# Two halves of the first weight block on one queue, and an activation load that waits for the identity

## The chip, the cores and the metric

The kernel runs on one core of a Trainium2 chip. A core has five engines with instruction streams of their own: TensorE (PE in the profile; its weight loads are PEld), VectorE (DVE), ScalarE (ACT), GpSimd (POOL) and SyncE (SP). SyncE and ScalarE issue the DMA transfers in this kernel, each on its own queue (SPq and ACTq in the profile). The metric is the time of one execution on the device in microseconds (us); lower is better. The median of three runs before the change is given below.

## The reference

The reference prunes the weight matrix 2:4 and multiplies: in each group of four consecutive rows of w, column by column, the two entries of largest magnitude are kept.

```python
# x: (16, 512, 1024), w: (1024, 1024), b: (1024,), all bf16
wg = w.reshape(G, M, D)                      # M = 4
mag = jnp.abs(wg)
order = jnp.argsort(mag, 1)
thr = jnp.take_along_axis(mag, order[:, M - N:M - N + 1, :], 1)   # N = 2
wp = (wg * (mag >= thr)).reshape(D, D)
return jnp.einsum("bsd,df->bsf", x, wp) + b
```

So there are 8192 tokens (64 tiles of 128), 1024 input features and 1024 output columns.

## The kernel before

**Tiles.** The contraction over 1024 features is cut into two groups g of 512; within a group, partition q holds four consecutive rows (m = 0 to 3) of w, so that one group of four lies in one partition and pruning is elementwise work on VectorE. `w_sb` is the raw weight, `wp` the pruned one in this layout, and `wp_nat` the pruned one in natural row order, which the DMA queues make from `wp` (calls `W0.0` and the like).

**The opening stage.** Weights are pruned in six pieces: four of 256 columns for g = 0, two of 512 columns for g = 1. Piece 0 is what everything starts with; its raw weights come as two loads of 128 KB, rows m = 0, 1 (first half) and m = 2, 3 (second half). While pieces are pruned, the first seven token tiles (0 to 6) are loaded in plain layout (`load_x`; tiles 3 and 4 are one load of 256 KB, 5 and 6 one, 2 one of 128 KB, 0 and 1 one), transposed on TensorE against an identity matrix (L193, tokens `T3a` and so on; four 128-column transposes to a tile), copied out of PSUM by ScalarE (L198, `C3a` and so on) and multiplied with each pruned piece as soon as it is there (L229, `M3.0yp`: tile 3, piece 0, rows y = m 2 and 3, columns p = the left half). Later tiles come transposed by DMA (L112, L237, L411) and use `wp_nat` (L242); these are 88% of the time.

**Pruning a piece** on VectorE: `abs` (L169, sign bit masked off; `abs0a` for the first half of piece 0, `abs0b` for the second), `hi` and `lo` (maximum and minimum within each of two pairs), `t1`, `t2` and `thr` (the second largest of the four), `mask` (`is_ge`) and `mult` (the write into `wp`). `hi0a` reads the pair that the first half holds, `hi0b` that of the second; `lo0` before the change does both pairs in one instruction. The `abs` of pieces 2 and 3 is done by ScalarE (L162), behind its copies.

**What sets the order.** Each engine's sequence in the opening is written out by hand in `order`, a list of tokens for each of "pe", "dve", "act" and "sp"; `run` emits them engine by engine, and `seq` keeps each engine's instructions in that sequence. Before that list, TensorE runs `filler` matmuls on constants that write a PSUM bank nobody reads: six of 512 columns and fourteen of 128 (L138). The transposes are next in TensorE's order, `T3a` first. The loads that stand ahead of the list are issued in the order of the calls, on SyncE by default and on ScalarE where the call says "act". ScalarE's first calculation is `spark` (L121), one element, which brings in its function table. `make_identity` (GpSimd) builds the identity.

Of the kernel before, what the change touches and what calls it, by code (L numbers as in the profile page):

```python
# [11 lines left out]
def kernel(  # L12
# [7 lines left out]
    nc = tc.nc  # L20
    P = 128
    bf16 = mybir.dt.bfloat16
# [32 lines left out]
    const = ctx.enter_context(tc.tile_pool(name="const", bufs=1))  # L55
# [11 lines left out]
    def seq(eng, inst):  # L67
        if eng in tails:
            tc.add_manual_dep(inst.ins, tails[eng].ins.name, NOSYNC, reason="program order")
        tails[eng] = inst  # L70
        return inst

    def pe(i):
        return seq("pe", i)
# [4 lines left out]
    def act(i):  # L79
        return seq("act", i)  # L80
# [4 lines left out]
    def pool(i):  # L85
        return seq("pool", i)
# [9 lines left out]
    def issue(eng, out_, in_):  # L96
        q = nc.sync if eng == "sp" else nc.scalar
        return seq(eng, q.dma_start(out_, in_))

    def load_w(g, c0, c1, ma=0, mb=4, eng="sp"):  # L100
        issue(eng, w_sb[:, g, ma:mb, c0:c1], wv[:, g, ma:mb, c0:c1])

    def load_x(ta, tb, eng="sp"):
        xs = const.tile([P, tb - ta, HK], bf16, name=f"x_{ta}")
        issue(eng, xs[:], xf[ta * P:tb * P, :HK].rearrange("(t p) k -> p t k", p=P))
        for t in range(ta, tb):
            x_sb[t] = xs[:, t - ta, :]
# [7 lines left out]

    xnat, held = {}, {}

    load_w(0, 0, 256, 0, 2)
    load_w(0, 0, 256, 2, 4, "act")
    load_x(5, 7, "act")  # L120
    act(nc.scalar.activation(spark[:], nc.const_aps.tensor(1.0, [P, 1], bf16), Act.Abs))  # L121
    load_x(3, 5)
    load_x(2, 3)
    load_w(0, 256, 512)
    load_x(0, 2)
    load_w(0, 512, 768)
# [2 lines left out]
    xnat.update(load_lead(0))  # L129
    pieces = [(0, 0, 256), (0, 256, 512), (0, 512, 768), (0, 768, 1024), (1, 0, 512), (1, 512, 1024)]  # L130

    ident = const.tile([P, P], bf16)
    make_identity(nc, ident[:])
    warm_ps = psum_o.tile([P, FH], fp32, name="ps")

    def filler(n, rep=1):
        for _ in range(n):
            pe(nc.tensor.matmul(warm_ps[:, :rep * P], lhsT=nc.const_aps.tensor(1.0, [P, P], bf16),  # L138
                                rhs=nc.const_aps.tensor(1.0, [P, rep * P], bf16), start=True, stop=True))
# [119 lines left out]
    def stage(key):  # L259
        solo = key[1] == "h"  # L260
        q, h, at = (pair_of[key[0]], key[2], int(key[0] != SOLO)) if solo else (key[0], key[1] // 2, key[1] % 2)
        if (q, h) not in staged:
# [12 lines left out]
        ),  # L275
        "dve": (
# [4 lines left out]
        ),  # L281
        "act": (
            "C3a C4a C5a C6a C2a S0b0 C0a C1a abs2 S3b0 S2b0 abs3 S0b1 U6h0 S3b1 S2b1 S0b2 S3b2 S2b2 S0b3 U6h1 S3b3 "
# [107 lines left out]
    def run(queues):  # L391
        while any(queues.values()):
            moved = False
            for eng, toks in queues.items():
                while toks and all(n in written for n in needs(eng, toks[0])):
                    emit(eng, toks[0])
                    tok = toks.pop(0)
                    written.add(tok)
                    if tok[0] == "M" or tok[0].islower():
                        written.update(atoms(tok))  # L400
                    moved = True
            assert moved, queues

    filler(6, 4)
    filler(14)
    run({eng: order[eng].split() for eng in order})

    def load_nat(ta, tb):
# [117 lines left out]
```

## Time and profile before

| What | us |
|---|---|
| median of three runs | 232.86 (232.36 to 233.05) |
| the profiled execution | 232.89 |
| its span, first to last instruction | 231.1 |
| TensorE busy in the span | 226.6 |
| VectorE busy | 107.9 |
| ScalarE busy | 14.0 |
| GpSimd busy | 17.6 |

The profile is of one execution. A row of its timeline gives the start in us from the beginning of the span, the us it lasted, the engine, the line of the kernel, the operation, what is written and read, and how often; several instructions of a kind in a row are merged into one line. What stands in brackets is how long the engine sat idle before and what ended that. Busy time of TensorE counts matmuls that overlap in its pipeline, so the pace is read from distances between starts. A DMA has two lines: one in the timeline, of the issuing engine's time, and one in the list of issues, with the us from issue to landing.

### The profile page before, as it was taken

The page shows a single profiled execution, that of the slowest core. Times are in us where ns is not written, and L with a number is a line of the kernel's source. Part 1 is how long each engine was busy: PE and PEld are TensorE (multiplying, and loading weights), DVE is VectorE, ACT ScalarE, POOL GpSimd, SP SyncE. Part 2 cuts the span into 40 slices and gives each one's busy share as a digit, 9 for nine tenths or more (in the row PEclk, how much of TensorE's full clock was granted, in tenths as well). Part 3 has the DMA queues.
Part 4 walks back from the last instruction along what each step waited for, and adds up shares of the span by engine and source line. Part 5 has one row for each costly group of instructions (what it writes and reads, how often), then busy time and mean ns, then how long its engine had stood idle before and what let it go on. Part 6 is the DMA issues. An engine that isn't in the chain of part 4 may idle for free.

```text
span 231.1 us, 2851 instructions
## 1 busy us (share of the span) xinstructions
PE 226.6 (98%) x1142; PEld 110.9 (48%) x1162; DVE 107.9 (47%) x200; ACT 14.0 (6%) x27; POOL 17.6 (8%) x15
## 2 busy tenths in 40 slices
PE   8999999999999999999999999999999999999995
PEld 5986444444444444444444444444444444444443
DVE  3999877844424424424424424423423423433434
ACT  2874100000000000000000000000000000000000
POOL 1000199700000000000000000000000000000000
PEclk9999999999999999999999999999999999999999
DMA  6999999997399422991259821693128932122122
GB/s 203 276 197 280 164 217 223 297 320 252 124 206 232 155 91 72 237 281 64 75 116 252 222 94 71 162 298 134 65 91 198 273 122 83 54 91 91 53 86 91
DMA packets 79308, 38.19 MB, mean 165 GB/s; under 512 B 64192, under 2 KB 71744, under 8 KB 79296
## 3 DMA queue, kind: packets, MB, share of 16 engines
q1 hardware_dynamic: 68384, 20.75, 43.6%
q10 hardware_dynamic: 10912, 17.27, 20.9%
q8 instruction: 9, 0.15, 0.3%
q14 instruction: 3, 0.02, 0.0%
HBM read 3.28 MB, written 16.78 MB: 87 GB/s over the span
## 4 chain that ended last, share of the span: by engine, by line
PE 98%; issue 0%; DVE 0%
PE ps L242 88%; PE ps L229 5%; PE tp L242 2%; PE ps L138 2%; PE tp L193 1%; PE ps L193 0%; DVE o L437 0%
## 5 line engine op out<-in xcount | busy, mean ns | idle before, releaser
L242 PE MATMUL ps<-wp_nat,xb 128*128 128x512 bf16 (+1 forms) x831 | 178.9, 375 | 0.9
L242 PEld LDWEIGHTS <-xb 128*128 128x128 bf16 x848 | 82.2, 98 | 97.7
L437 DVE TENSOR_TENSOR o<-ps,bias_sb 128x512 bf16<-128x512 f32 (+1 forms) x112 | 71.6, 677 | 113.7 <-PE ps L242 111.4
L433 POOL TENSOR_TENSOR st<-st,bias_sb 128x1024 f32<-128x1024 f32 x8 | 16.7, 2142 | 0.0
L242 PE MATMUL ps<-wp_nat,xlead 128*128 128x512 bf16 x63 | 14.7, 379 | 0.1
L242 PEld LDWEIGHTS <-xlead 128*128 128x128 bf16 x88 | 8.6, 98 | 10.2
L229 PE MATMUL ps<-wp,xt 128*128 128x256 bf16 (+1 forms) x130 | 12.8, 258 | 0.0
L439 DVE TENSOR_TENSOR o<-ps,st 128x512 bf16<-128x512 f32 x16 | 11.1, 691 | 2.8 <-PE ps L242 2.2
L229 PEld LDWEIGHTS <-xt 128*128 128x128 bf16 x130 | 10.9, 98 | 1.1
L242 PE MATMUL ps<-wp_nat,xlow 128*128 128x512 bf16 x47 | 10.6, 379 | 0.1
L264 ACT COPY st<-ps 128x512 f32<-128x512 f32 x14 | 7.4, 600 | 3.2 <-PE ps L229 3.1
L242 PEld LDWEIGHTS <-xlow 128*128 128x128 bf16 x48 | 4.7, 98 | 5.7
L159 DVE TENSOR_TENSOR mag<-mag,hi 128x256 bf16<-128x256 bf16 (+2 forms) x15 | 6.1, 435 | 0.1
L159 DVE TENSOR_TENSOR wp<-w_sb,mag 128x256 bf16<-128x256 bf16 (+2 forms) x15 | 6.1, 435 | 0.1
L242 PE MATMUL tp<-wp_nat,xlead 128*128 128x512 bf16 x23 | 5.8, 380 | 0.0
L138 PE MATMUL ps<-const-bfloat16-1.0 128*128 128x128 bf16 (+1 forms) x20 | 4.2, 408 | 0.8 <-PEq L510 0.8
L169 DVE TENSOR_SCALAR mag<-w_sb 128x512 uint16<-128x512 uint16 (+2 forms) x5 | 2.3, 473 | 3.5 <-DMA w_sb<-in_w_dram 3.5
L138 PEld LDWEIGHTS <-const-bfloat16-1.0 128*128 128x128 bf16 x20 | 2.3, 146 | 2.4 <-issue 2.4
L159 DVE TENSOR_TENSOR hi<-mag 128x512 bf16<-128x512 bf16 (+2 forms) x7 | 3.2, 458 | 0.1
L159 DVE TENSOR_TENSOR lo<-mag 128x512 bf16<-128x512 bf16 (+1 forms) x6 | 3.1, 509 | 0.0
L193 PEld LDWEIGHTS <-x 128*128 128x128 bf16 x28 | 2.3, 124 | 0.3 <-DMA x<-in_x_dram 0.2
L422 POOL COPY pruned<-wp 128x1 bf16<-128x1 bf16 x1 | 0.2, 187 | 26.7 <-DVE wp L159 26.7
(18 smaller groups left out, 18.8 us busy)
## 6 DMA issues: line engine op xcount, KB each, us to landing
out_dram<-o ACTq DMA_DIRECT2D x58, 256.0 KB, 2.4
wp_nat<-wp SPq DMA_DIRECT2D x14, 128.0 KB, 3.2
out_dram<-o ACTq DMA_DIRECT2D x10, 128.0 KB, 1.7
w_sb<-in_w_dram SPq DMA_DIRECT2D x2, 512.0 KB, 5.5
w_sb<-in_w_dram SPq DMA_DIRECT2D x3, 256.0 KB, 5.1
x<-in_x_dram SPq DMA_DIRECT2D x2, 256.0 KB, 4.3
x<-in_x_dram ACTq DMA_DIRECT2D x1, 256.0 KB, 4.0
bias_sb<-in_b_dram SPq DMA_DIRECT2D x1, 256.0 KB, 4.7
```

The source lines that it names most:

```text
L138: pe(nc.tensor.matmul(warm_ps[:, :rep * P], lhsT=nc.const_aps.tensor(1.0, [P, P], bf16), rhs=nc.const_aps.tensor(1.0, [P, rep * P], bf16), ...
L159: dve(nc.vector.tensor_tensor(out, a, b_, op=op))
L169: dve(nc.vector.tensor_single_scalar(mag.bitcast(u16), w_.bitcast(u16), 0x7FFF, op=Alu.bitwise_and))
L193: pe(nc.tensor.transpose(tp[:, m, :], xg[:, m, :], ident[:]))
L229: pe(nc.tensor.matmul(ps[:, c0 + d:c1 + d], lhsT=xpk[t][:, m, :], rhs=wp[:, g, m, c0:c1], start=(new and m == ms.start), stop=(left[key] = ...
L242: pe(nc.tensor.matmul(ps, lhsT=xt[:, kt - koff, :], rhs=wp_nat[:, kt, c0:c1], start=(kt == first), stop=(kt == last)))
L264: act(nc.scalar.copy(staged[(q, h)][:, at, :, :].rearrange("p t c -> p (t c)"), ps_open.pop(key)[:]))
L422: pool(nc.gpsimd.tensor_copy(out=pruned[:], in_=wp[:, 1, 3, Dout - 1:]))
L433: pool(nc.gpsimd.tensor_tensor(st[:], st[:], bias.to_broadcast([P, 2, 2, CW]), op=Alu.add))
L437: dve(nc.vector.tensor_tensor(o[:, c0:c1], ps, bias_sb[:, c0:c1], op=Alu.add))
L439: dve(nc.vector.tensor_tensor(o[:, c0:c1].rearrange("p (n c) -> p n c", n=2), ps.rearrange("p (n c) -> p n c", n=2), add, op=Alu.add))
```

## The change

Five things are edited.

- The second half of piece 0's weights is loaded on SyncE's queue, right behind the first half, and no longer on ScalarE's.
- ScalarE's loads are now those of tiles 3 and 4 and of tile 2, and both stand behind `spark`; the load of tiles 5 and 6 goes to SyncE. Thus SyncE issues: first half, second half, tiles 5 and 6, piece 1, tiles 0 and 1, pieces 2 and 3, and the first of g = 1.
- Before the load of tiles 3 and 4, GpSimd copies one column of the identity into the tile that the load will fill; the identity is built ahead of the loads for that.
- VectorE's order for piece 0 begins `abs0a hi0a abs0b lo0a lo0b hi0b`: one instruction more, and `hi0a` ahead of the second half's `abs`.
- Three of the fourteen short fillers are gone.

```diff
     def load_x(ta, tb, eng="sp"):
         xs = const.tile([P, tb - ta, HK], bf16, name=f"x_{ta}")
+        if ta == 3:
+            pool(nc.gpsimd.tensor_copy(out=xs[:, 0, :1], in_=ident[:, :1]))
         issue(eng, xs[:], xf[ta * P:tb * P, :HK].rearrange("(t p) k -> p t k", p=P))
...
+    ident = const.tile([P, P], bf16)
+    make_identity(nc, ident[:])
     load_w(0, 0, 256, 0, 2)
-    load_w(0, 0, 256, 2, 4, "act")
-    load_x(5, 7, "act")
+    load_w(0, 0, 256, 2, 4)
     act(nc.scalar.activation(spark[:], nc.const_aps.tensor(1.0, [P, 1], bf16), Act.Abs))
-    load_x(3, 5)
-    load_x(2, 3)
+    load_x(3, 5, "act")
+    load_x(5, 7)
+    load_x(2, 3, "act")
     load_w(0, 256, 512)
...
-    ident = const.tile([P, P], bf16)
-    make_identity(nc, ident[:])
...
-            "abs0a abs0b hi0a lo0 hi0b t20 t10p t10q thr0p thr0q ..."
+            "abs0a hi0a abs0b lo0a lo0b hi0b t20 t10p t10q thr0p thr0q ..."
...
     filler(6, 4)
-    filler(14)
+    filler(11)
```

8 rows, old and new, of the table order are left out of this document.

## The prediction

> **What bounds the kernel now.** I read the page first (shares and the chain that ended last), then the waits of the whole run, then TensorE's timeline of the opening.
>
> ```profile
> span 231.1 us, 2851 instructions
> PE 226.6 (98%) x1142; PEld 110.9 (48%) x1162; DVE 107.9 (47%) x200; ACT 14.0 (6%) x27; POOL 17.6 (8%) x15
> PE 98%; issue 0%; DVE 0%
> ...
> PE ps L138 <- PEq L510: 0.8, 1, 0.8
> PEld L193 <- DMA x<-in_x_dram: 0.2, 1, 0.2
> ```
>
> The chain is TensorE from one end to the other. In the list of all waits TensorE stands twice: 0.8 us at the start of the program, and 0.2 us before its first transpose, for a load of x. After that transpose it waits for nothing until the end. So a delay of that transpose shifts the end by as much, and so does a gain, as long as no other wait appears.
>
> ```profile
> 0.77 4.21 PE L138 MATMUL ps<-const-bfloat16-1.0 128*128 128x512 bf16 x20 [0.77 <-PEq L510]
> 4.96 1.04 PE L193 MATMUL tp<-ident,x 128*128 128x128 bf16 x8
> 5.80 0.72 PE L193 MATMUL ps<-ident,x 128*128 128x128 bf16 x8
> 6.35 0.39 PE L193 MATMUL tp<-ident,x 128*128 128x128 bf16 x4
> 6.58 1.92 PE L229 MATMUL ps<-wp,xt 128*128 128x128 bf16 x20
> 3.29 1.43 PEld L138 LDWEIGHTS <-const-bfloat16-1.0 128*128 128x128 bf16 x13 [0.28 <-issue]
> 4.96 1.62 PEld L193 LDWEIGHTS <-x 128*128 128x128 bf16 x20 [0.24 <-DMA x<-in_x_dram]
> ```
>
> Two things are to be seen. Fillers end and the load of tiles 3 and 4 lands (1.24 plus 3.7, rows below) at 4.9, and the transposes start at 4.96. And the pace changes: the first eight transposes start within 0.84 us (5.80 less 4.96, 0.105 each), the last four within 0.23 (0.0575 each). The eight between take 0.55: x at 0.105 and 8-x at 0.0575 gives x of about 2. So ten transposes, 1.05 us, ran at about half clock, and the full clock came at 6.0, some 5.2 us after the first filler. Each us of work at the slow pace costs 0.45 us (1 less 0.0575/0.105); these cost 0.48.
>
> **The change, part by part: ScalarE's load.** The order of the built program tells more than the diff. Its rows for the new kernel:
>
> ```
> ACT  L124 LoadActFuncSet
> ACT  L124 Activation spark<-const-bfloat16-1.0 128x1
> ACT  L98 DMACopy x_91<-in_x_dram 128x2x512 [waits DMAHW1_49,Pool_49]
> ACT  L98 DMACopy x_96<-in_x_dram 128x512 [waits DMAHW2_49]
> DVE  L171 TensorScalarPtr mag_145<-w_sb 128x512 [waits DMAHW1_49]
> PE   L195 Ldweights x_3_91 [waits DMAHW1_49,Pool_49]
> ```
>
> Eight completion semaphores (0 to 7) are dealt out to the loads in turn. SyncE's first eight loads take all eight, since the wait for the identity puts ScalarE's loads behind them, and none of the eight waits. The load of tiles 3 and 4 then gets number 1 again, the one for which the second `abs` (the fifth row) waits: that of the second weight half. So it waits for GpSimd's copy and also for the landing of that half. Tile 2's load gets number 2 and waits for tiles 5 and 6, which are SyncE's third.
>
> ```profile
> 0.73 0.45 SPq L98 DMA_DIRECT2D w_sb<-in_w_dram  x1
> 1.24 0.96 SPq L98 DMA_DIRECT2D x<-in_x_dram  x2
> 2.25 0.68 SPq L98 DMA_DIRECT2D w_sb<-in_w_dram  x1
> 0.74 0.50 ACTq L98 DMA_DIRECT2D w_sb<-in_w_dram  x1
> 1.26 0.49 ACTq L98 DMA_DIRECT2D x<-in_x_dram  x1
> 1.79 1.28 ACT L121 ACT_TABLE_LOAD   x1 [1.79 <-issue]
> 1.01 0.29 POOL masks.py:199 TENSOR_SCALAR_AFFINE_SELECT ident<-ident 128x128 bf16<-128x128 bf16 x1
> w_sb<-in_w_dram SPq DMA_DIRECT2D x1, 128.0 KB, 2.7
> w_sb<-in_w_dram ACTq DMA_DIRECT2D x1, 128.0 KB, 2.9
> x<-in_x_dram SPq DMA_DIRECT2D x1, 256.0 KB, 3.7
> x<-in_x_dram ACTq DMA_DIRECT2D x1, 256.0 KB, 4.0
> out_dram<-o ACTq DMA_DIRECT2D x58, 256.0 KB, 2.4
> ...
> 2.60:4.78 2.18, 2.18 (x17) 1.58 (x14) 1.28 (x6) 0.68 (x2) 0.00 (x0) 1.00 1.02 345
> ```
>
> The issue rows are those of the single loads: the weight halves at 0.73 and 0.74 took 2.7 and 2.9 us, tiles 3 and 4 at 1.24 took 3.7, tiles 5 and 6 at 1.26 took 4.0. The windows row ends with the bytes that all queues moved: 345 GB/s.
>
> *Release.* GpSimd's copy is no limit: the identity is done at 1.30, and the table load, now first on ScalarE at 0.74, ends near 2.0. The second half is issued at 1.24, where the x load stood; with its 2.7 us it lands at 3.94. On the other side, both halves had landed by 3.64 (0.74 plus 2.9) with the same bytes, and the first at about 3.5 (below). I take 3.7, nearer the second, because no x is now ahead of it; ends 3.5 and 3.94.
>
> *Flight.* A load of 256 KB issued at that point meets SyncE's backlog (six loads behind the halves). The first half's 2.7 us holds 128 KB; the other 128 KB cost 0.38 us at 345 GB/s and 0.76 at half of it. So 3.1 to 3.5, and I take 3.3. Ends: the 2.4 of a store of that size, and the 4.0 of ScalarE's load.
>
> Tiles 3 and 4 thus land at 3.7 + 3.3 = 7.0 (ends 5.9 and 7.9), where the first transpose started at 4.96: **+2.04 us**. The fillers are over by then, and nothing else stands ahead in TensorE's order: `T5a`, whose load may be there, is queued behind `T3a`.
>
> *Tile 2.* Tiles 5 and 6 landed at 5.3 (1.26 plus 4.0); with 256 KB fewer ahead of them (0.76 us at 345 GB/s) about 4.5. Tile 2 then needs 2.7 for 128 KB: 7.2, or 8.0 if no byte is saved. Its transpose is due sixteen transposes after 7.0, at 7.9 at the fast pace. I take 0; ends 0 and 0.1.
>
> **Fillers.** Thirteen took 1.43 us, so three are 0.33 us, and TensorE would be free at about 4.5. In front of the landing at 7.0 that gains nothing; before the change, too, the load ended that wait. Their price is in the clock: work stops after 3.7 us of it (0.77 to 4.5), where the full clock had come after 5.2. If the clock is full when the transposes start, the 0.48 us come back: **-0.48**. If it isn't, see the second rival.
>
> **VectorE's order.**
>
> ```profile
> 3.50 0.49 DVE L169 TENSOR_SCALAR mag<-w_sb 128x512 uint16<-128x512 uint16 x2 [3.50 <-DMA w_sb<-in_w_dram]
> 4.11 0.42 DVE L159 TENSOR_TENSOR lo<-mag 128x512 bf16<-128x512 bf16 x1
> 4.45 0.28 DVE L159 TENSOR_TENSOR hi<-mag 128x256 bf16<-128x256 bf16 x1
> 4.65 0.28 DVE L159 TENSOR_TENSOR lo<-lo 128x256 bf16<-128x256 bf16 x1
> 5.80 0.48 DVE L159 TENSOR_TENSOR wp<-w_sb,mag 128x256 bf16<-128x256 bf16 x2
> 7.01 0.42 DVE L169 TENSOR_SCALAR mag<-w_sb 128x1024 uint16<-128x1024 uint16 x1
> 9.47 1.06 ACT L162 ACTIVATE mag<-w_sb 128x1024 bf16<-128x1024 bf16 x1
> 10.56 0.43 DVE L159 TENSOR_TENSOR lo<-mag 128x512 bf16<-128x512 bf16 x1
> ```
>
> The whole `lo0` occupies 0.34 us until the next start, a half-size step 0.20: two halves cost 0.40, so +0.06. If the second half lands at 3.94, `abs0b`, `lo0a`, `lo0b`, `hi0b` follow at 0.20 each, and `t20` starts at 4.74 instead of 4.65: +0.09 at most. An earlier first half can give about as much back. The first product is written at 5.80 to 6.1, and TensorE's first matmul on it moves from 6.58 to above 8: two us of cover, so I cost this at 0 (without the cover, 0.09).
>
> Piece 1's weights keep their issue slot at 2.25, so `abs1` at 7.01 stands. From piece 2 on VectorE is tied to TensorE: its `lo2` at 10.56 follows ScalarE's `abs2` (9.47 plus 1.06), which stands behind ScalarE's copies of transposed tiles and so moves with them. Both sides shift together: no further cost, no recovery.
>
> **Sum.** 232.89 (the profiled execution, 0.03 above the median) + 2.04 - 0.48 = 234.45, given as 234.4.
>
> **Rivals.**
>
> *The clock is not open when the transposes start.* TensorE idles from 4.5 to 7.0, and the first 1.8 us of fillers had not opened it (they lay before 2.6, and the pace stayed slow). Then between 1.05 us of work, as before, and 5.2 us, the whole count anew, run slowly; in the middle 3.1. At 0.45 that is 1.40, less the 0.48 already in the old time: 232.89 + 2.04 + 0.92 = 235.9 (234.9 to 236.8). Against it: 3.7 us of fillers may be enough.
>
> [...]
>
> *The landing is cheap.* Release at 3.5 and the store's 2.4 us: transposes at 5.9, 232.89 + 0.94 - 0.48 = 233.35, within 0.3% of the time before. Against it: no load of the opening took under 2.7 us, even for half the bytes.
>
> *Faster, by an earlier full clock.* If the gate opens during the fillers, all twenty transposes run fast, and 0.48 us are won. It decides if tiles 3 and 4 start before 4.96 + 0.48 = 5.44; for 0.3% faster before 4.74, and at 4.6 it gives 232.05. The release at 3.5 or later leaves 1.1 us for 256 KB; the shortest row is 2.4. I see little for it.
>
> *The wait does nothing.* If the semaphore is long met when ScalarE gets there (by 2.2), the load lands at 2.2 + 3.1 = 5.3 and the time is 232.89 + 0.34 - 0.48 = 232.75: no change. Against it: VectorE's first `abs` waited for weights until 3.50.
>
> **How the numbers follow.** A measurement of this kernel tells about 0.3% (0.7 us) from no change. Forecast as reckoned, 233.6 to 234.9: 0.50. Clock still shut, 234.9 to 236.8: 0.33. A late flight beside a shut clock, beyond 236.8: 0.03. Cheap landing: 0.06. Faster: 0.04. The wait does nothing: 0.04. So faster 0.04, same 0.10 (the cheap landing and the idle wait), slower 0.86. The range goes from 233.5 to 236.6: it leaves out the last two cases, most of the cheap landing, and the upper end of the shut clock.
>
> **What would show it.** Right: the first transpose starts near 7.0, its wait of about 2.5 us ended by the DMA of x; ScalarE's issue of that load stands near 3.7, right behind the start of VectorE's second `abs`; no later wait of TensorE. The clock shows in the transposes' spacing: 0.0575 or 0.105. Wrong: ScalarE's issue near 2, a first transpose before 5.5, or a later gap on TensorE where VectorE or tile 2 comes too late.

## The result, and the profile after

The changed kernel takes 239.14 us (median of four runs, 238.28 to 239.56) against 232.72 for the kernel before: 2.75% slower, the ratio being 1.0275 with a 95% interval of 1.0255 to 1.0296. The profiled execution took 238.28, with a span of 236.5. The direction was forecast; the 234.4 us were not, and the time lies above the range.

The page's shares and chain of the changed kernel, then rows from the list of its waits:

```profile
span 236.5 us, 2869 instructions
PE 95%; DMA 3%; SPq 0%; issue 0%; DVE 0%; ACTq 0%
...
PE tp L195 <- DMA x<-in_x_dram: 4.7, 1, 4.7
DVE lo L161 <- ACT mag L164: 5.6, 1, 5.6
```

DMA is now 3% of the chain that ended last, and TensorE waits 4.7 us for a load of x before its first transpose. There is no other new wait of TensorE. VectorE's 5.6 us before piece 2's `lo` is the tie to ScalarE's `abs2`: it has the time to spare.

TensorE's timeline of the opening, with ScalarE's DMA issues and the issue-to-landing rows of the loads issued at 0.73, 1.24, 1.75, 2.25, 2.97 (SyncE) and 3.54 (ScalarE; these are single loads, one at a time):

```profile
0.78 3.89 PE L140 MATMUL ps<-const-bfloat16-1.0 128*128 128x512 bf16 x17 [0.78 <-PEq L512]
9.40 1.02 PE L195 MATMUL tp<-ident,x 128*128 128x128 bf16 x8 [4.73 <-DMA x<-in_x_dram]
10.21 1.06 PE L195 MATMUL ps<-ident,x 128*128 128x128 bf16 x8
11.06 0.63 PE L195 MATMUL tp<-ident,x 128*128 128x128 bf16 x4
11.49 2.44 PE L231 MATMUL ps<-wp,xt 128*128 128x128 bf16 x20
13.76 0.39 PE L195 MATMUL tp<-ident,x 128*128 128x128 bf16 x4
3.54 1.54 ACTq L98 DMA_DIRECT2D x<-in_x_dram  x2
w_sb<-in_w_dram SPq DMA_DIRECT2D x1, 128.0 KB, 2.3
w_sb<-in_w_dram SPq DMA_DIRECT2D x1, 128.0 KB, 2.2
x<-in_x_dram SPq DMA_DIRECT2D x1, 256.0 KB, 3.0
w_sb<-in_w_dram SPq DMA_DIRECT2D x1, 256.0 KB, 3.4
x<-in_x_dram SPq DMA_DIRECT2D x1, 256.0 KB, 5.1
x<-in_x_dram ACTq DMA_DIRECT2D x1, 256.0 KB, 5.7
```

The second weight half, issued at 1.24, lands at 3.46, and ScalarE issues the load of tiles 3 and 4 at 3.54. That is the semaphore wait. The load then flies 5.7 us, to 9.26, and the first transpose starts at 9.40 where it had started at 4.96: 4.44 us. All twenty transposes run at 0.106 us each, and so does the work behind them until 12.55, when the clock opens; 3.15 us are slow, where 1.05 were before. The 2.10 more cost 0.45 each, 0.95. Together 5.39, which is the whole difference of the two profiled executions (238.28 less 232.89).

The median lies 0.9 above this execution. Each run's span comes with its mean granted clock. It is 1.0 for this run, in which nothing was recorded before the clock opened at 12.55, and 0.986 for the other three: by an estimate from that mean (1.4% of 237.5 us, twice) some 6.7 us at half clock. Run e4 below, with the same mean, shows such a course in a trace.

### The profile page after: what moved, and what is told of

The parts are those of the page before. It is cut to its first block, busy times and chain, and to the rows that moved or that the text cites. A ratio compares the mean times of both kernels' runs of the same rounds, so it can differ in the third digit from the quotient of the medians.

```text
span 236.5 us, 2869 instructions
## 1 busy us (share of the span) xinstructions
PE 228.3 (97%) x1159; PEld 111.7 (47%) x1159; DVE 108.0 (46%) x201; ACT 14.3 (6%) x27; POOL 17.8 (8%) x16
## 4 chain that ended last, share of the span: by engine, by line
PE 95%; DMA 3%; SPq 0%; issue 0%; DVE 0%; ACTq 0%
PE ps L244 86%; PE ps L231 5%; DMA x<-in_x_dram 2%; PE tp L244 2%; DMA w_sb<-in_w_dram 1%; PE tp L195 1%; PE ps L195 0%; SPq L98 0%; DVE o L439 0%; ACTq L98 0%
## 5 line engine op out<-in xcount | busy, mean ns | idle before, releaser
L244 PE MATMUL ps<-wp_nat,xb 128*128 128x512 bf16 (+2 forms) x848 | 179.8, 375 | 0.0
L231 PE MATMUL ps<-wp,xt 128*128 128x256 bf16 (+1 forms) x130 | 13.3, 264 | 0.0
L231 PEld LDWEIGHTS <-xt 128*128 128x128 bf16 x130 | 11.5, 102 | 1.2
L195 PE MATMUL tp<-ident,x 128*128 128x128 bf16 x16 | 2.0, 288 | 4.7 <-DMA x<-in_x_dram 4.7
L161 DVE TENSOR_TENSOR lo<-mag 128x512 bf16<-128x512 bf16 (+2 forms) x7 | 3.1, 459 | 5.7 <-ACT mag L164 5.6
```

The source lines that it names most:

```text
L161: dve(nc.vector.tensor_tensor(out, a, b_, op=op))
L195: pe(nc.tensor.transpose(tp[:, m, :], xg[:, m, :], ident[:]))
L231: pe(nc.tensor.matmul(ps[:, c0 + d:c1 + d], lhsT=xpk[t][:, m, :], rhs=wp[:, g, m, c0:c1], start=(new and m == ms.start), stop=(left[key] = ...
L244: pe(nc.tensor.matmul(ps, lhsT=xt[:, kt - koff, :], rhs=wp_nat[:, kt, c0:c1], start=(kt == first), stop=(kt == last)))
```

## The experiments

All edits are of the changed kernel unless said otherwise. The medians of the kernel before, taken beside them, were 232.45 (the first four), 232.44 (the next four) and 232.76 (the last three).

**e1: without the copy, and so without the wait**

```diff
-        if ta == 3:
-            pool(nc.gpsimd.tensor_copy(out=xs[:, 0, :1], in_=ident[:, :1]))
```

> The changed kernel without GpSimd's copy into the tile of 3 and 4. The built order then gives ScalarE's load of tiles 3 and 4 a fresh semaphore and no wait; everything else of the change stays. Theory 1 (the reused semaphore is the cause: the load waited until 3.5 for the second weight half): the load is issued at about 2.2 us, behind the table load, lands 3.1 to 4.0 us later, first transpose between 5.3 and 6.2, time 233.0 to 235.0, depending on the clock. Rival (putting that load on ScalarE's queue behind the table load, or the DVE order, is the cause, and the wait is incidental): first transpose still after 8, time still above 237.5.

Measured: 233.57 us, ratio 1.0045 (1.003 to 1.006), within the range expected. ScalarE's and TensorE's rows, VectorE's second `abs`, and the loads issued at 0.80 (ScalarE) and 1.25 (SyncE):

```profile
0.73 1.28 ACT L122 ACT_TABLE_LOAD   x1 [0.73 <-PEq L510]
0.80 0.98 ACTq L98 DMA_DIRECT2D x<-in_x_dram  x2
4.46 0.97 PE L193 MATMUL tp<-ident,x 128*128 128x128 bf16 x8
5.88 0.64 PE L193 MATMUL ps<-ident,x 128*128 128x128 bf16 x8 [0.45 <-DMA x<-in_x_dram]
7.32 1.92 PE L229 MATMUL ps<-wp,xt 128*128 128x128 bf16 x20 [0.58 <-DVE wp L159]
5.02 0.29 DVE L169 TENSOR_SCALAR mag<-w_sb 128x512 uint16<-128x512 uint16 x1 [0.75 <-DMA w_sb<-in_w_dram]
x<-in_x_dram ACTq DMA_DIRECT2D x1, 256.0 KB, 3.4
w_sb<-in_w_dram SPq DMA_DIRECT2D x1, 128.0 KB, 3.8
```

5.6 us of the loss go with the wait. Two steps behind the expected time failed, both usefully. ScalarE did not issue its load at 2.2 but at 0.80, while the table load was running (0.73 to 2.01): here the table load, of 1.28 us, didn't hold up the DMA issue that stands behind it. And the load, issued 0.45 us before the second weight half on the other queue, landed 0.8 us ahead of it (4.2 against 5.0; the second half took 3.8 us instead of 2.2). VectorE's second `abs` waits until 5.02, and TensorE waits 0.58 us for the first pruned weights. The place taken early in the line was the second half's. So the time fell into its range by two misses that offset each other: the transposes began at 4.46 and not at 5.3 or later, and TensorE then waited 0.45 and 0.58 us.

**e2: 40 more fillers.** `filler(40)` behind `filler(11)`.

> The changed kernel with 40 more short fillers, so that TensorE goes on working until about 7.5 to 8.7 us and the load of tiles 3 and 4 still lands last (9.3 us). The wait isn't touched. Theory (3.15 us of the work after the first transpose ran at half clock because TensorE stood idle from 4.5 to 9.4): the clock is full at the first transpose, the transposes are 0.056 us apart, and 0.45 x 3.15 = 1.4 us come back: 237.7 us. Rival (the clock's opening doesn't hang on the fillers): transposes at 0.105 us, time 239.1.

Measured: 237.32 us (236.78 to 238.64), ratio 1.0196 (1.0178 to 1.0214). That is near the 237.7, but the one trace doesn't show the course expected. It is of the slowest execution (238.64): the clock opens at 3.68, the fillers end at 6.63 (8.55 less 1.92), the first transposes stand at 8.55 at the fast pace (0.056 us apart), and at 10.50 the clock is taken back:

```profile
8.55 0.61 PE L195 MATMUL tp<-ident,x 128*128 128x128 bf16 x8 [1.92 <-DMA x<-in_x_dram]
10.48 0.61 PE L195 MATMUL tp<-ident,x 128*128 128x128 bf16 x4 [0.87 <-DMA x<-in_x_dram]
0.27:3.68 3.41, 2.91 (x10) 1.00 0.47 105
7.09:10.50 3.41, 1.08 (x17) 1.00 1.10 330
10.50:13.92 3.42, 3.42 (x23) 0.50 1.21 232
```

The last three rows are windows: length, TensorE's busy us, matmul count, granted clock, DMA share and GB/s. (The profile gives 1.00 also for the time before the first recorded opening.) This execution's mean clock is 0.993; the other four, 236.78 to 237.43 us, have 0.999 or 1.0, so none of them records such a stretch of 3.4 us at half clock. They may well have kept the clock, as expected; no trace of them shows it. In addition tile 2 is late, see e9.

**e3 and e4: what makes the flight long.** Both release the load by data: the copy into its tile reads the second weight half, not the identity. e3 holds back SyncE's loads of pieces 2 to 4 and the first transposing load, by a GpSimd copy from tile 3 into piece 2's weights; e4 holds only the transposing load, by one into `xlead`.

```diff
-            pool(nc.gpsimd.tensor_copy(out=xs[:, 0, :1], in_=ident[:, :1]))
+            pool(nc.gpsimd.tensor_copy(out=xs[:, 0, :1], in_=w_sb[:, 0, 3, :1]))
...
+    pool(nc.gpsimd.tensor_copy(out=w_sb[:, 0, 0, 512:513], in_=x_sb[3][:, :1]))
     load_w(0, 512, 768)
```

This is e3; e4 has, in place of the last edit:

```diff
+    pool(nc.gpsimd.tensor_copy(out=xlead[:, 0, P:P + 1], in_=x_sb[3][:, :1]))
     xnat.update(load_lead(0))
```

> The changed kernel with the load of tiles 3 and 4 released by the second weight half through data (GpSimd copies one column of that half, not of the identity, into the tile), so the release stays at 3.5 to 3.9 us; and SyncE's later loads (pieces 2, 3, 4 and the first transposing load) held back until tiles 3 and 4 have landed, by a GpSimd copy from tile 3 into piece 2's weights. Theory (the 5.7 us flight is SyncE's backlog): flight 2.4 to 3.5 us, first transpose at 6.3 to 7.3, time 235 to 237. Rival (ScalarE's queue is slow by itself, or one of the 16 DMA engines is): flight 5 us or more, first transpose at 9 or later, time 238.5 or more.

> As the run before, but only the first transposing load of SyncE's queue is held back until tiles 3 and 4 have landed; the three weight loads ahead of it stay. Release by the second weight half through data. If the transposing load causes the long flight: first transpose at 6.5 to 7.5. If the plain weight loads cause it: first transpose at 9 or later, time about 239.

Measured, one run each: e3 236.81 us, flight 4.1, first transpose at 8.05; e4 238.81 us, flight 4.8, first transpose at 8.78. Both first transposes lie between the forecasts. So the transposing load is not the cause, and SyncE's loads issued behind ours account for a part at most: without any of them the flight was still 4.1 us. The windows of e4, and for comparison two of the changed kernel:

```profile
0.63:4.04 3.41, 3.27 (x14) 1.00 0.57 152
4.04:7.45 3.41, 0.39 (x6) 1.00 1.00 257
7.45:10.86 3.41, 2.08 (x20) 0.50 1.05 328
10.86:14.28 3.42, 3.42 (x23) 0.50 1.10 215
```

```profile
2.31:5.72 3.41, 2.36 (x14) 1.00 0.98 251
9.14:12.55 3.41, 3.15 (x29) 1.00 1.18 227
```

In e4 the clock opened at 4.04 during the fillers, was taken back at 7.45 in the wait, and came again only at 14.28, after 5.5 us of slow work. That is a run with two half-clock stretches of 3.41 us; its mean clock is 0.986, as in the three runs above.

**e7: the same place in the line, on the other queue.** No copy, no wait; tiles 3 and 4 are SyncE's sixth load, tile 2 its seventh.

> Tiles 3 and 4 issued on SyncE as the sixth load, at about 3.6 us (where ScalarE issued it in the changed kernel), with no wait and no copy; tile 2 behind it. Theory A (place in the line of issue sets the landing, not the queue): flight 3.4 us or more, first transpose at 7.0 to 8.5, time 235 to 238. Rival B (ScalarE's queue was the slow one): flight under 3.0 us, as SyncE's third load had in the changed kernel, first transpose before 6.6.

Measured: 237.2 us (one run), as forecast for the place in the line. The load, issued at 3.62, and the transposes:

```profile
x<-in_x_dram SPq DMA_DIRECT2D x1, 256.0 KB, 4.6
8.26 1.04 PE L193 MATMUL tp<-ident,x 128*128 128x128 bf16 x8 [3.59 <-DMA x<-in_x_dram]
```

A flight of 4.6 and a start at 8.26: as late as from ScalarE (e3 8.05, e4 8.78) with no semaphore in play. So, with issues at 3.62 us from SyncE (flight 4.6) and at 3.81 from ScalarE (e3, flight 4.1), it is the moment of issue that makes the landing late, not ScalarE's queue.

**e5: the wait for the identity kept, the reused semaphore avoided**

```diff
+    pool(nc.gpsimd.tensor_copy(out=w_sb[:, 0, 0, 512:513], in_=ident[:, :1]))
     load_w(0, 512, 768)
```

> The changed kernel with one more GpSimd copy, of a column of the identity into piece 2's raw weights, ahead of SyncE's load of that piece. That load is issued at 3.6 anyhow, so the copy delays nothing, but now only five SyncE loads stand ahead of ScalarE's load of tiles 3 and 4 in the dealing of semaphores: it gets a fresh one and waits for the identity copy alone. Theory A (the whole loss is the reused semaphore; and loads of both queues are served as one line in the order of issue): issue at 1.6, third or fourth in the line, landing at 4.3 to 4.8, first transpose at 4.5 to 4.8, VectorE's second half not later than 3.8, time 231.9 to 232.7, that is the time before or a little less. Rival B (a load on ScalarE's queue behind the table load and beside SyncE's queue is slow in itself): landing at 5.5 or later, time 233.3 or more.

Measured: 232.99 us (232.72 to 236.6, twelve runs), ratio 1.0037 (1.0014 to 1.006). 6.15 us of the 6.7 are gone, by nothing but another number in the dealing of semaphores. The median lies between the two forecasts (232.7 at most, 233.3 at least). The profile fell on one of the three runs above 235 (235.16): the load, issued at 1.59, took 4.2 us, the first transpose stood at 5.95, and the clock opened at 9.76. So the landing forecast of 4.3 to 4.8 is not confirmed by a trace; the nine runs below 233.3 were faster, but where the load landed in them is not shown.

```profile
1.59 0.50 ACTq L98 DMA_DIRECT2D x<-in_x_dram  x1
5.95 1.02 PE L196 MATMUL tp<-ident,x 128*128 128x128 bf16 x8 [1.28 <-DMA x<-in_x_dram]
2.94:6.35 3.41, 2.13 (x18) 1.00 1.03 292
```

**e10: e5 with the three fillers back.** `filler(14)`.

> The run with the fresh semaphore, with the three fillers put back (fourteen). If the missing fillers leave an idle stretch in which the clock opens late, the runs above 235 go and the median falls to 232.4 to 232.7. If they cost nothing: 233.0 as without them, with the same spread.

Measured: 233.45 us (233.21 to 235.47), ratio 1.0044 (1.0022 to 1.0066), with two of ten runs above 235. No gain over e5 (1.0037), so the three fillers weren't the matter. Its trace, of a run of 233.23, has the load at 1.58 flying 3.6 us, to 5.2, and the first transpose at 5.29: later than the 4.3 to 4.8 as well.

**e6: everything on SyncE, tiles 3 and 4 third, no copy and no wait**

> All first loads on SyncE in a row: first half, second half, tiles 3 and 4, tiles 5 and 6, tile 2, piece 1, tiles 0 and 1; no copy from the identity, no wait; VectorE's order and the eleven fillers as in the changed kernel. Theory A (one line in the order of issue): tiles 3 and 4, issued third at 1.75, land at 4.4 to 4.8, second half at 3.5, first transpose at 4.5 to 4.8, time 231.9 to 232.6. If landing were set by the issuing queue's own load: tiles 3 and 4 later than before's 4.92, since three loads share one queue, and time 232.7 or more.

Measured: 233.23 us, ratio 1.0025 (1.0015 to 1.0036). Tiles 3 and 4 came as forecast (first transpose at 4.70), the time did not: SyncE issues its loads 0.5 to 0.7 us apart (0.73, 1.24, 1.75, 2.25, 2.97 and 3.62 in the changed kernel), tiles 0 and 1 are now its seventh load instead of its fifth, and TensorE waits for them until 8.65.

```profile
4.70 0.64 PE L193 MATMUL tp<-ident,x 128*128 128x128 bf16 x8 [0.50 <-DMA x<-in_x_dram]
5.59 0.64 PE L193 MATMUL ps<-ident,x 128*128 128x128 bf16 x8 [0.25 <-DMA x<-in_x_dram]
8.65 0.41 PE L193 MATMUL tp<-ident,x 128*128 128x128 bf16 x4 [0.44 <-DMA x<-in_x_dram]
0.10:3.51 3.41, 2.74 (x9) 1.00 0.37 96
```

**e8: the kernel before with VectorE's new order and eleven fillers**

> The kernel before with two edits of the change alone: VectorE's order for piece 0 and three fillers fewer. As costed: VectorE 0.06 us later on piece 0 under 0.5 us of cover, the fillers hidden by the load of tiles 3 and 4 at 4.92: the time before within 0.3%, 232.1 to 232.9. Rival: the shorter activity opens the clock one stage later, up to 1 us slower.

Measured: 232.63 us against 232.44, ratio 1.0004 (0.9995 to 1.0013). These two edits cost and bring nothing.

**e9: 70 more fillers**

> The changed kernel with 70 more short fillers: forty ended at 6.4 us once the clock was open, so TensorE stood idle again for 2.1 us and the clock was taken back; seventy reach to about 9. The waits stay. Theory (the clock follows how busy TensorE was in windows of 3.4 us): the clock opens before 8, stays open, no transpose at 0.105, tiles 3 and 4 landing at 8.4 to 9.3 as before; time 232.4 - 0.48 + (8.6 to 9.4 less 4.97), that is 235.6 to 236.4. Rival (the clock is lost at the wait whatever TensorE does): 238.5 to 239.5.

Measured: 237.31 us (237.08 to 237.64), ratio 1.0201 (1.018 to 1.0222). The clock part came as expected: it opened at 3.67 and stayed open. The time was 0.9 us above the upper end of the forecast because I had left a term out:

```profile
8.66 0.61 PE L195 MATMUL tp<-ident,x 128*128 128x128 bf16 x8 [0.27 <-DMA x<-in_x_dram]
9.11 0.61 PE L195 MATMUL ps<-ident,x 128*128 128x128 bf16 x8
10.61 0.41 PE L195 MATMUL tp<-ident,x 128*128 128x128 bf16 x4 [0.89 <-DMA x<-in_x_dram]
x<-in_x_dram ACTq DMA_DIRECT2D x1, 128.0 KB, 5.8
```

Tile 2's load, held by the other reused semaphore and issued at 4.76, lands at 10.56. At the fast pace its transposes, due 0.45 us after 9.11, wait 1.05 us for it. At the slow pace of the changed kernel they are due at 11.06, and the wait is hidden. With it the profiled execution adds up: 232.89 - 0.48 + 3.70 (8.66 less 4.96) + 1.05 = 237.16, which is what it took.

**e11: the changed kernel once more**

> The changed kernel once more, for a second trace of it. If the flight of 5.7 us is what that place in the line costs: 5.5 to 6.0 us again, first transpose at 9.2 to 9.6. If the last of the sixteen DMA engines is late by chance: between 4.6 and 5.7 us, first transpose between 8.2 and 9.4. ScalarE's issue at 3.5 to 3.7 in both.

Measured: 238.19 us (one run), issue at 3.62, flight 5.0, first transpose at 8.76, clock open at 12.82, and 0.23 us of wait for tile 2. The order of loads in e2, e9, e11 and the first trace is the same; the flights were 4.8, 5.0, 5.0 and 5.7. In the first trace's records of the load's sixteen completions six of the DMA engines are done by 6.86, ten by 7.70, fifteen by 8.27 and the last at 9.26. So up to 0.9 us of the flight changes from run to run with the order unchanged, and in the first trace the last engine alone is 1.0 us behind.

## Why the prediction was wrong

**TensorE sets the end, and a shift of its first transpose passes to the end whole:** right. The shift and the slow stretch make up the difference of the profiled executions.

**The reused semaphore:** right, and the heart of the loss. Release was forecast at 3.7 and came at 3.46; e5 removes only this and keeps 0.4% of the 2.75%.

**Flight, 3.3 us: the step that failed in size.** I let the load share the bytes with SyncE's backlog at half rate. The runs show something near one line in the order of issue across both queues. In e1 the weight half, issued later, landed later although it stood on the other queue; in e7 the same moment of issue on SyncE gave the same late landing. Ahead at 3.54 were tiles 5 and 6, piece 1 and tiles 0 and 1, which landed at 4.70, 5.61 and 8.06. The packets say how the 5.7 us divide. SyncE's queue is q1, ScalarE's q10 (up to 11 us q10 moves 0.39 MB in the changed kernel, the 256 and 128 KB of ScalarE's two loads). The rows give packets, MB and busy share; they are of the changed kernel from 3.54 to 5.63 (first row) and from there to 9.27 (two rows), and of e3 from 5.72 to 7.92, which is the same part of its load's flight (q10's bytes include tile 2's):

```profile
q1 hardware_dynamic: 880, 0.60, 99.9%
q1 hardware_dynamic: 1188, 0.69, 65.0%
q10 hardware_dynamic: 389, 0.37, 32.4%
q10 hardware_dynamic: 416, 0.39, 61.9%
q1 hardware_dynamic: 47, 0.04, 5.2%
```

For the first 2.1 us the load moved no byte, while SyncE's earlier loads moved 0.60 MB; the program's first load, with nothing ahead, had needed 1.1 us (0.73 to 1.83) to its first packet. The other 3.6 us it shared with SyncE's queue, which moved 0.69 MB meanwhile. In e3, with SyncE's later loads held, the two parts are 1.9 and 2.2 us. So some 1.4 us of the second part go with the loads behind it and the late last engine. The whole flight was 5.7 us here, 4.8 and 5.0 in e2 and e11 with the order of loads unchanged, and 4.1 in e3: by these the loads behind cost some 0.7 to 0.9 of the 1.6, as an estimate, and the rest is that run's own. The order is not strict: tile 2, issued at 4.72, landed at 10.18, before a load that SyncE had issued at 4.22 (6.8 us). The term is 2.4 us too small (4.44 against 2.04).

**The clock, -0.48: the step that failed in kind.** I took it that a clock opened by the fillers would still be open at 7.0, and gave 0.33 to the other case, with 3.1 us of slow work in the middle of its bounds. That case came, with 3.15 us: +0.95, so 1.43 more than the sum. That 3.15 stands so near 3.1 is luck: the slow work behind the first transpose was 2.9 us in e3, 4.1 in e11 and 5.5 in e4. No trace in which TensorE stood idle for some 3.6 us or more before the first transpose (3.58 in e3, 3.59 in e7, 4.09 in e11, 4.35 in e4, 4.73 in the first) had the full clock there. In e3, e4 and e7 the fillers were enough to open it, at 4.0 to 4.7, but it was taken back at 7.4 to 8.1; in the two traces of the changed kernel it opened only at 12.55 and 12.82. With TensorE kept at work (e9: 0.27 us idle before the first transpose) it stayed open.

Both terms together, 2.40 and 1.43, are the 3.83 between the 234.45 of the sum and the 238.28 of the profiled execution. I had priced the two failures as rivals of each other, and here they are one chain: the late landing is the wait in which the clock is lost. Their joint case had 0.03.

**Tile 2, 0:** right for the changed kernel only by luck, because the slow clock hid it; forecast to land at 7.2, it landed at 10.18.

**Fillers and VectorE's order, 0:** right (e8). VectorE's `t20` started at 4.43 instead of 4.65, and from piece 2 on it moved with TensorE: `lo` at 15.99, right behind ScalarE's `abs2` (14.89 plus 1.06).

```profile
4.43 0.29 DVE L161 TENSOR_TENSOR lo<-lo 128x256 bf16<-128x256 bf16 x1
14.89 1.06 ACT L164 ACTIVATE mag<-w_sb 128x1024 bf16<-128x1024 bf16 x1
15.99 0.43 DVE L161 TENSOR_TENSOR lo<-mag 128x512 bf16<-128x512 bf16 x1 [5.63 <-ACT mag L164]
```

**The rival in which the wait does nothing** rested on ScalarE being busy until 2.2 with its table load. e1 shows the issue at 0.80: ScalarE was there 2.7 us before the second half landed (3.46).

## What to carry to other kernels

Read the built program's waits, not only the diff: a load that moves behind others in the dealing of completion semaphores can inherit a wait for a transfer that it has nothing to do with (issue at 3.54 us, without the wait at 0.80 in e1), and one more copy elsewhere can undo it (e5, issue at 1.59). Count a late-issued load behind what was issued before it on any queue (here the flight grew from 3.7 us, issued at 1.24, to between 4.1 and 5.7, issued at 3.54 to 3.81), and price an idle stretch of TensorE together with the clock that it can lose (here 3.58 us idle or more, with 2.9 to 5.5 us at the slow pace behind it). A transfer gained early was taken from another (in e1 the second weight half took 3.8 us instead of 2.2): none of the orders tried here was faster than the kernel before.

## What the runs showed of the hardware

The clock changed, wherever a trace has several changes, at distances of 3.41 us or twice that (e2: 3.68, 10.50, 13.92; e3: 4.11, 7.52, 10.94; e4: 4.04, 7.45, 14.28; e7: 4.66, 8.07, 11.49). The stretches below are 3.41 us long, counted back or on from such a change. Of those measured, the stretch before an opening had TensorE busy for 2.74 us at the least (e6; then 2.89 in e3 and 2.91 in e2). Behind stretches with 2.08 (e4), 2.13 (e5) and 2.36 us (changed kernel, 2.31 to 5.72) the clock was not opened. Behind stretches with 0.01 (e7), 0.36 (e3), 0.39 (e4) and 1.08 us (e2) the open clock was taken back; behind one with 2.37 us (e9, 7.08 to 10.49) it stayed open. No run was made to settle what decides.

What stays open is why the sixteen DMA engines finish one load so far apart: from 6.74 to 9.26 us in the changed kernel's first trace, and from 4.40 to 4.92 for the same load in the kernel before. No run was made to settle it.
